# First three batches by halves of d_ff, float64 weights converted in pairs, G in float32 on quarters of the array

## The chip, the core and the metric

The kernel runs on one core of a Trainium2 chip. The core has five engines with a queue each: TensorE (PE in the profile, its weight loads PEld), VectorE (DVE), ScalarE (ACT), GpSimd (POOL) and SyncE (SP), which here issues every DMA. The metric is the device time of one execution in microseconds (us); less is better.

## The reference

Inputs are float64 weights and float32 activations. Eight batches b of 512 tokens, 8 heads of 64, and 32 state rows per head and batch:

```python
scores  = scale * x @ state.T                 # per batch and head
xread   = softmax(scores)  @ state            # 512 token rows a batch
sread   = softmax(scores.T) @ x               # 32 state rows a batch
x1 = concat([xread, sread])                   # 8 * 544 rows of 512
y  = relu(x1 @ w_in1)**2 @ w_out1             # d_ff = 2048, "MoE 1"
out = silu(y @ w_in2) @ w_out2                # "MoE 2"
```

## The kernel before, in words

**Folding.** For the token rows the kernel never forms xread. It multiplies the state by the first weight: G = state @ w_in1 per batch and head, so that x1 @ w_in1 becomes softmax(scores) @ G. The softmaxed scores, transposed, are the pages AThi/ATlo; G's are Ghi/Glo. Accurate products are made from float32r halves: hi*hi + hi*lo + lo*hi, three matmuls in place of one.

**Weights.** They come as pairs of 32-bit words (the float64's halves, int32 page `raw`). A piece is 128 rows by 512 columns, its raw page 512 KB. `c_load` fetches it, `c_abs` (ACT) and `c_bits` (five DVE instructions of 512 columns: three TENSOR_SCALAR, two SCALAR_TENSOR_TENSOR) rebuild two float32 parts a and c in the page `cv`, and `c_split` (one ACT cast, two TENSOR_TENSOR) makes hi and lo of their sum. For the second MoE's weights `c_sum` adds a and c and `c_store` keeps the float32 sum in DRAM. Each 512 x 2048 weight is 16 pieces. The first weight is converted twice, the second time (`w1s`, its rows in another order) for the state rows.

**G.** `g_unit(i)` takes piece i (column block q = i // 4, row block p = i % 4) and four block matrices `sp` of the state (128 x 128, half of it zeros, built hi and lo by `sp_build`). For each `sp`, which serves two batches, three float32r matmuls of 512 columns go to one PSUM bank; ACT or DVE copies it to the page `go`. G of batches 0 and 1 goes straight into their Glo pages by DMA, that of 2 to 7 to DRAM (`g_d`), from where `G_load` fetches it and `G_split` (ACT cast, DVE subtraction of 1024 columns) makes hi and lo.

**Stage A** has 144 slots, (batch j, block c of 128 columns of d_ff): j = 0 to 7 with 512 tokens each, and j = 8 with the 256 state rows. In a slot `gemm1` makes h in psC (6 matmuls for a token batch), `chain_a` makes relu and square and splits it (`rg`, `gact`: ACT, one DVE subtraction), and two slots later `gemm2` adds it into the four banks psA and psB (4 x 3 matmuls). So a token slot has 18 matmuls of 512 columns. After a batch's 16 slots `evac_a` copies the four banks out. Scores of a batch take two float32 matmuls a half g for batch 0 (`sblkf`), and six float32r ones (`sblk`, `x_split`) for the others; softmax work and the read of the state rows (`sread`) are spread over earlier and later slots. Batches 0 and 1 have their `sread` put off to slots 16 to 26.

**Stages after A** multiply by the second MoE's weights in a seven-product scheme (`gemm3`, `gemm4`); the change does not touch them.

**Order.** Nothing is issued as written. Each call is recorded by the class `Plan` (`record`, line 140; all instructions therefore show line L184) with an estimated cost (`cost`, line 107). `order` plays the program through with these costs, picks by urgency among the operations of the next 25 slots, respects the 50 pages of 128 x 1024 float32 in SBUF, and `emit` issues the result. Every engine then runs its own queue in that fixed order. `arith` may go to DVE or POOL and `copy` to ACT or DVE, as the plan decides. Functions that the change touches: `cost` 107, `c_load` to `sched_conv` 479 to 531, `g_unit` 571, `G_load` 596, `scores` 624, `sread_evac` 738, `gemm2` 772, `evac_a` 783, `sched_attention` 1067, `init` 1089, and the schedule in lines 1101 to 1176.

## Time and profile before

| | us |
|---|---|
| median of 3 runs | 1411.97 |
| lowest and highest run | 1406.2, 1414.91 |
| the profiled execution, its own time | 1404.88 |
| its span, first to last instruction | 1403.0 |

The profiled execution is 7.1 us (0.5%) under the median, and 1.9 us of its time lie outside the span. The profile's first part gives each engine's busy time; "windows" give it for stretches of the span, with instruction counts; groups of instructions give a mean duration; the order of time ("timeline") merges neighbours of one kind and gives in brackets what ended an idle stretch before them. The durations of instructions on one engine overlap a little, and a matmul's recorded duration runs from its start to the modelled end of its pipeline, so the distance between starts is what one costs in a stream. PEclk is the granted TensorE clock, 1.00 being 2.4 GHz.

### The profile page before, as it was taken

The page shows a single profiled execution, that of the slowest core. Times are in us where ns is not written, and L with a number is a line of the kernel's source. Part 1 is how long each engine was busy: PE and PEld are TensorE (multiplying, and loading weights), DVE is VectorE, ACT ScalarE, POOL GpSimd, SP SyncE. Part 2 cuts the span into 40 slices and gives each one's busy share as a digit, 9 for nine tenths or more (in the row PEclk, how much of TensorE's full clock was granted, in tenths as well). Part 3 has the DMA queues.
Part 4 walks back from the last instruction along what each step waited for, and adds up shares of the span by engine and source line. Part 5 has one row for each costly group of instructions (what it writes and reads, how often), then busy time and mean ns, then how long its engine had stood idle before and what let it go on. Part 6 is the DMA issues. An engine that isn't in the chain of part 4 may idle for free. (4 is left out here: it accounts for less than half of the span.)

```text
span 1403.0 us, 21067 instructions
## 1 busy us (share of the span) xinstructions
PE 1360.8 (97%) x7764; PEld 1187.9 (85%) x7764; DVE 1059.6 (76%) x1711; ACT 728.8 (52%) x1156; POOL 46.0 (3%) x41
## 2 busy tenths in 40 slices
PE   6888899999999999999999999999999999999998
PEld 3566688888888888888997888998889999999998
DVE  8999997888888888888888867777887444445443
ACT  8875674655565655566762534244555333333331
POOL 2000000000000000000021000000100000000000
PEclk9999999999999999999999999999999999999999
DMA  9981152545464636541738966677899666665563
GB/s 359 367 323 45 40 148 76 172 136 180 128 186 126 198 103 196 167 166 44 241 111 305 363 226 233 243 245 263 296 329 333 218 198 220 214 191 193 188 191 110
DMA packets 205943, 283.20 MB, mean 202 GB/s; under 512 B 12432, under 2 KB 147088, under 8 KB 205840
## 3 DMA queue, kind: packets, MB, share of 16 engines
q1 hardware_dynamic: 205840, 281.85, 60.6%
q8 instruction: 61, 1.00, 0.3%
q14 instruction: 42, 0.34, 0.1%
HBM read 165.54 MB, written 112.07 MB: 198 GB/s over the span
## 5 line engine op out<-in xcount | busy, mean ns | idle before, releaser
L184 ACT ACTIVATE rg<-psC 128x512 f32<-128x512 f32 (+1 forms) x144 | 82.4, 574 | 178.3 <-PE psC L184 177.0
L184 DVE TENSOR_TENSOR gact<-rg,gact 128x512 fp32r<-128x512 f32 (+1 forms) x142 | 93.3, 657 | 25.8 <-ACT rg L184 23.5
L184 DVE SCALAR_TENSOR_TENSOR cv<-raw,cv 128x512 int32<-128x512 int32 (+1 forms) x160 | 109.4, 688 | 0.9
L184 PE MATMUL psC<-AThi,Ghi 128*128 128x512 f32 x256 | 100.6, 398 | 2.3 <-ACT rg L184 1.7
L184 DVE TENSOR_SCALAR cv<-cv 128x512 int32<-128x512 int32 (+1 forms) x240 | 98.0, 426 | 4.4 <-ACT cv L184 3.4
L184 PE MATMUL psC<-AThi,Glo 128*128 128x512 f32 x256 | 100.0, 395 | 0.0
L184 PE MATMUL psC<-ATlo,Ghi 128*128 128x512 f32 x256 | 99.5, 393 | 0.0
L184 ACT ACTIVATE gact<-rg 128x512 fp32r<-128x512 f32 (+1 forms) x144 | 87.6, 608 | 3.4
L184 PEld LDWEIGHTS psC<-AThi,Ghi 128*128 128x128 f32 x256 | 47.9, 188 | 15.6 <-ACT rg L184 4.3
L184 ACT ACTIVATE cv<-raw 128x512 f32<-128x512 f32 x80 | 53.0, 671 | 8.4 <-DMA raw<-in_w_dram 5.5
L184 PEld LDWEIGHTS psC<-AThi,Glo 128*128 128x128 f32 x256 | 48.0, 188 | 10.8 <-DVE Glo L184 0.4
L184 PEld LDWEIGHTS psC<-ATlo,Ghi 128*128 128x128 f32 x256 | 48.1, 188 | 10.5
L184 DVE TENSOR_TENSOR rg<-rg 128x512 f32<-128x512 f32 (+1 forms) x52 | 34.3, 660 | 27.6 <-ACT rg L184 27.1
L184 ACT ACTIVATE rg<-rg 128x512 f32<-128x512 f32 (+1 forms) x92 | 54.8, 595 | 0.0
L184 ACT ACTIVATE r<-r 128x1024 f32<-128x1024 f32 (+2 forms) x20 | 18.7, 933 | 62.2 <-DVE r L184 54.9
L184 DVE TENSOR_TENSOR W<-psC,U 128x512 f32<-128x512 f32 (+2 forms) x40 | 24.1, 609 | 25.3 <-PE psC L184 25.2
L184 DVE TENSOR_TENSOR Glo<-Glo,Ghi 128x1024 fp32r<-128x1024 f32 x32 | 39.0, 1218 | 1.1 <-ACT Ghi L184 1.0
L184 ACT ACTIVATE W<-W 128x1024 f32<-128x1024 f32 (+2 forms) x20 | 18.7, 933 | 36.8 <-DVE W L184 31.6
L184 ACT ACTIVATE U<-U 128x512 f32<-128x512 f32 (+2 forms) x36 | 28.6, 796 | 14.1 <-DVE U L184 13.9
L184 ACT ACTIVATE r<-psA 128x512 f32<-128x512 f32 (+2 forms) x40 | 20.8, 533 | 28.5 <-PE psA L184 28.4
L184 DVE TENSOR_TENSOR U<-psB,U 128x512 f32<-128x512 f32 (+2 forms) x40 | 23.8, 606 | 13.9 <-PE psB L184 10.8
L184 ACT CAST Ghi<-Glo 128x1024 fp32r<-128x1024 f32 x32 | 33.4, 1045 | 0.5 <-DMA g<-go 0.5
(1422 smaller groups left out, 4575.4 us busy)
## 6 DMA issues: line engine op xcount, KB each, us to landing
raw<-in_w_dram SPq DMA_DIRECT2D x64, 512.0 KB, 6.4
t<-s SPq DMA_DIRECT2D x36, 512.0 KB, 5.2
Glo<-g SPq DMA_DIRECT2D x48, 256.0 KB, 4.4
t<-r SPq DMA_DIRECT2D x24, 512.0 KB, 4.4
xTr<-in_xT_dram SPq DMA_DIRECT2D x16, 512.0 KB, 5.7
g<-go SPq DMA_DIRECT2D x16, 512.0 KB, 6.5
xnr<-in_xN_dram SPq DMA_DIRECT2D x16, 512.0 KB, 5.1
x<-yt SPq DMA_DIRECT2D x32, 256.0 KB, 4.0
```

Source lines behind the costliest of these rows:

```text
L184: lambda engine=engine, method=method, a=a, k=k: getattr(engine, method)(*a, **k)))
```

## The change

It does the following, all in the preparation and in stage A.

1. The slots of batches 0, 1, 2 run in two parts: c 0 to 7 of batch 0, 1, 2 (slots 0 to 23), then c 8 to 15 of the same (24 to 47); from slot 48 on batches 3 to 8 as before. After a first part `evac_part` copies the four banks into two pages, after the second `y_add` adds the banks to them (4 DVE additions instead of copies).
2. Conversions work on two pieces at once: 1024-column pages a and c. Where DVE reads the raw words (SCALAR_TENSOR_TENSOR) and in `c_abs` it stays at 512 columns an instruction.
3. The first weight is not split: `c_sum` makes it one float32 page. `g_unit` multiplies it with the float32 state as loaded, in 64 x 64 quarters: per unit 8 float32 matmuls (64 rows, 64 columns of weights, 512 columns moving) at the array positions (0,0), (64,64), (0,64), (64,0). The `sp` matrices go. Column blocks q = 0, 1 (units 0 to 7) are made ahead of slot 0, blocks q = 2, 3 (units 8 to 15) at slot 17, between batch 1's and batch 2's first part, since they use the banks psA and psB.
4. The converted first weight is stored in DRAM (`w1_d`, 8 x 512 KB) and fetched and split for the state rows, in place of the second conversion.
5. Scores of batches 1 and 2 also go in float32 (two matmuls a half), without `x_split` and `sblk`.
6. `sread` of batches 0, 1, 2 is put off to slots 34 to 50; `w3`/`w4` conversions, in pairs, to slots 50 to 134. A unit's Glo pieces are sent by 4 DMAs instead of 2, `G_load` takes 4 instead of 2, `sread_evac` 8 transposes of 32 x 32 instead of 4 of 32 x 64.
7. The plan's cost takes a quarter matmul at a fourth.

```diff
-            return max(n / 2.4 + 13, 109) * (4 if args["rhs"].dtype == F32 else 1)
+            share = 4 if args.get("tile_position") else 1
+            return max(n / 2.4 + 13, 109) * (4 if args["rhs"].dtype == F32 else 1) / share
...
-    A_END = (B + 1) * NC
     N_PAGE, N_QUAD = 50, 10
+    NB, ST, PARTS = 3, 34, ((0, 8), (8, 16))
...
+    w1_d = [dram_tile([P, 1024], f"w1d{i}") for i in range(NC // 2)]
...
-    g_d = [[dram_tile([4 * P] + k + [512], f"g{i}{q}") for q in range(4)] for i, k in enumerate(([], [2]))]
+    g_d = [[dram_tile([4, P] + k + [512], f"g{i}{q}") for i, k in enumerate(([], [2]))] for q in range(4)]
...
+    def c_load(key, srcs):
+        raws[key] = [page("raw", I32) for _ in range(2)]
+        for t, src in zip(raws[key], srcs):
+            D.dma_start(t, src)
...
+        a = page("cv", F32)
+        for k in range(2):
+            A.activation(out=a[:, k * 512:(k + 1) * 512], in_=words(key, k)[1].bitcast(F32), func=AF.Abs)
...
+        a, c = cv[key], page("cc", F32)
+        ai, ci = a.bitcast(I32), c.bitcast(I32)
...
         V.tensor_scalar(out=a, in0=a, scalar1=UP_LO, scalar2=UP_HI, op0=ALU.max, op1=ALU.min)
...
+        for k in range(2):
+            h = slice(k * 512, (k + 1) * 512)
+            V.scalar_tensor_tensor(out=ci[:, h], in0=words(key, k)[1], scalar=-0x40000000, in1=ai[:, h],
+                                   op0=ALU.bitwise_and, op1=ALU.bitwise_or)
...
+        V.tensor_scalar(out=ai, in0=ci, scalar1=-0x800000, scalar2=None, op0=ALU.bitwise_and)
+        for k in range(2):
+            h = slice(k * 512, (k + 1) * 512)
+            V.scalar_tensor_tensor(out=a[:, h], in0=words(key, k)[0].bitcast(U32), scalar=2.0 ** -52, in1=a[:, h],
+                                   op0=ALU.mult, op1=ALU.mult)
...
-    def c_sum(key):
+    def c_sum(key, into=None):
         a, c = cv[key]
         arith(ALU.add, c, c, a)
         cv[key] = c
+        if into is not None:
+            into[key] = c
...
+        hi, lo = page(f"hi{key}"), page(f"lo{key}")
+        split_into(hi, c, c)
+        arith(ALU.add, lo, c, a)
+        into[key] = (hi, lo)
...
+    def sched_conv(key, srcs, s, into=None, dst=None, ahead=3, whole=False):
+        at(s - ahead, "dma", c_load, key, srcs)
         at(s - 1, "vec2", c_abs, key)
         at(s, "vec", c_bits, key)
-        if into is None:
-            at(s + 1, "vec", c_sum, key)
+        if into is None or whole:
+            at(s + 1, "vec", c_sum, key, into)
...
-    sp = [page(f"sp{i}") for i in range(4)]
-    sblkf = quad("sblkf")
+    sblkf = [quad(f"sblkf{b}") for b in range(NB)]
...
-        pg = w1p[("w1", i)]
-        rows = slice(p * P, (p + 1) * P)
-        for bp in range(4):
-            t = acc_tile(bp)
-            for k, (so, mo) in enumerate(((0, 0), (512, 0), (0, 512))):
-                T.matmul(out=t, lhsT=sp[bp][:, so + p * P:so + (p + 1) * P], rhs=pg[:, mo:mo + 512],
-                         start=k == 0, stop=k == 2)
-            if bp % 2 == 0:
-                o2 = page(f"go{i}{bp}", F32)
-            o = o2[:, bp % 2 * 512:(bp % 2 + 1) * 512]
-            copy(o, t)
+        pg = w1p[("w1", i // 2)][:, i % 2 * 512:(i % 2 + 1) * 512]
+        for bp in range(0, 4, 2):
+            ts = [acc_tile(bp), acc_tile(bp + 1)]
+            for k in range(2):
+                for r in range(2):
+                    ps, co = slice(r * 64, (r + 1) * 64), 64 * (r ^ k)
+                    T.matmul(out=ts[k][co:co + 64], lhsT=st[ps, bp + k, p].rearrange("p e n -> p (e n)"),
+                             rhs=pg[ps], start=True, stop=True, tile_position=(r * 64, co))
+            o2 = page(f"go{i}{bp}", F32).rearrange("p (k f) -> p k f", k=2)
+            for k in range(2):
+                copy(o2[:, k], ts[k])
             if bp == 0:
                 for b in range(2):
                     if (b, q) not in gp:
                         gp[(b, q)] = [None, page(f"Glo{b}{q}")]
-                    D.dma_start(gp[(b, q)][1][l * 64:(l + 1) * 64, g * 512:(g + 1) * 512].bitcast(F32),
-                                o[(b ^ l) * 64:((b ^ l) + 1) * 64])
-            elif bp == 1:
-                D.dma_start(g_d[0][q][rows], o)
-            elif bp == 3:
-                D.dma_start(g_d[1][q][rows], o2.rearrange("p (b f) -> p b f", b=2))
+                    for r in range(2):
+                        D.dma_start(f32(gp[(b, q)][1])[l * 64 + r * NS:l * 64 + (r + 1) * NS, g * 512:(g + 1) * 512],
+                                    o2[r * 64 + b * NS:r * 64 + (b + 1) * NS, 0])
+                D.dma_start(g_d[q][0][p], o2[:, 1])
+            else:
+                D.dma_start(g_d[q][1][p], o2)
+
+    def w1_store(i):
+        D.dma_start(w1_d[i], w1p.pop(("w1", i)))
+
+    def w1_load(i):
+        w1p[("s", i)] = split_page(f"w1s{i}", 1024, lambda lo: D.dma_start(lo, w1_d[i]))
     def G_load(b, q):
         lo = page(f"Glo{b}{q}")
-        src = g_d[b // 4][q]
-        src = (src[:, b // 2 % 2] if b >= 4 else src).rearrange("(g l e p) f -> l e p g f", g=2, l=2, e=2)
+        bp, e = divmod(b, 2)
+        src = g_d[q][1][:, :, bp % 2] if bp > 1 else g_d[q][0]
         for l in range(2):
-            D.dma_start(lo[l * 64:(l + 1) * 64, :].bitcast(F32).rearrange("p (g f) -> p g f", g=2),
-                              src[l, (b % 2) ^ l])
+            for r in range(2):
+                ro = (r ^ bp % 2) * 64 + e * NS
+                po = l * 64 + r * NS
+                D.dma_start(f32(lo)[po:po + NS].rearrange("p (g f) -> p g f", g=2),
+                            src.rearrange("(g l) x f -> l x g f", l=2)[l, ro:ro + NS])
         gp[(b, q)] = [None, lo]
...
-        if b == 0:
+        if b < NB:
             for l in range(2):
                 c0 = (2 * g + l) * P
-                T.matmul(out=t, lhsT=sblkf[:, c0:c0 + P], rhs=x[:, l * 512:(l + 1) * 512],
+                T.matmul(out=t, lhsT=sblkf[b][:, c0:c0 + P], rhs=x[:, l * 512:(l + 1) * 512],
...
         for h in range(4):
-            ps = slice(h * NS, (h + 1) * NS)
-            V.transpose(out=srT[ps, 2 * g:2 * g + 2, b * NS:(b + 1) * NS],
-                        in_=t[ps, h * 64:(h + 1) * 64].rearrange("p (e d) -> p e d", e=2))
-
-
-    gact, acc, yq = {}, {}, {}
+            for e in range(2):
+                ps = (h % 2) * 64 + e * NS
+                V.transpose(out=srT[ps:ps + NS, 2 * g + h // 2, b * NS:(b + 1) * NS],
+                            in_=t[h * NS:(h + 1) * NS, h * 64 + e * NS:h * 64 + (e + 1) * NS])
...
+        w = w2p[("w2", c // 2)]
...
+                T.matmul(out=acc[j][d][:, :n], lhsT=w[k][:, o:o + P], rhs=pg[:, s:s + n],
...
+    def y_copy(j, n):
+        ys = [page("y", F32)[:, :2 * n].rearrange("p (k n) -> p k n", k=2) for _ in range(2)]
+        for d in range(4):
+            copy(ys[d // 2][:, d % 2], acc[j][d][:, :n])
+        return ys
+
+    def evac_part(j):
+        if j in y_part:
+            y_add(j)
+        else:
+            y_part[j] = y_copy(j, S)
+        del acc[j]
+
+    def y_add(j):
+        for d in range(4):
+            y = y_part[j][d // 2][:, d % 2]
+            V.tensor_tensor(out=y, in0=acc[j][d], in1=y, op=ALU.add)
...
+        if j in y_part:
+            y_add(j)
+            ys = y_part.pop(j)
+        else:
+            ys = y_copy(j, n)
...
+        if b >= NB:
+            if g == 0:
+                at(s, "vec", sblk_build, b)
+            at(s, "vec", x_split, b, g)
+        elif g == 0:
+            at(s, "vec", s_put, b, sblkf[b], slice(0, 4, 3))
...
-        sched_conv(("w1", i), w_in_piece(w1, i), i - 19, w1p, ahead=3)
...
+    steps = [(b, c) for c0, c1 in PARTS for b in range(NB) for c in range(c0, c1)]
+    steps += [(b, c) for b in range(NB, B + 1) for c in range(NC)]
+    place = {x: s for s, x in enumerate(steps)}
...
+    for i in range(NC // 2):
+        q, p = divmod(i, 2)
+        if q < PARTS[0][1] // 4:
+            n = 2 * i - 4 * (PARTS[0][1] // 4) - 2
+            k = n - 3
+        else:
+            part = [u for u, (c0, c1) in enumerate(PARTS) if c0 <= 4 * q < c1][0]
+            n = slot(NB - 1, PARTS[part - 1][0]) + 1
+            k = n - 9 + 2 * p
+        sched_conv(("w1", i), w_in_pair(w1, i), k, w1p, whole=True)
+        at(max(n, k + 3) + 1, "late", w1_store, i)
         if i == 0:
-            at(-22, "dma", load_st, 0, B)
-        at(i - 16, "pe", g_unit, i)
-    for i in range(4):
-        at(-18, "vec", sp_build, i)
-    at(-14, "vec", s_put, 0, sblkf, slice(0, 4, 3))
+            at(-12, "dma", load_st)
+        at(n, "pe", g_unit, 2 * i)
+        at(n, "pe", g_unit, 2 * i + 1)
...
-        sched_conv(("w2", c), w_out_piece(w2, c), c - 1, w2p, ahead=5)
...
+    for i in range(NC // 2):
+        sched_conv(("w2", i), w_out_pair(w2, i), slot(0, 2 * i) - 1, w2p, ahead=5)
     for g in range(2):
-        sched_attention(1, g, 2 + 5 * g, True)
-        for b, s in ((0, 16), (1, 24)):
-            at(s + 2 * g - 1, "vec2", sm2_exp, b, g)
-            sched_sread(b, g, s + 2 * g)
-    for b in range(2):
+        for b in range(1, NB):
+            sched_attention(b, g, slot(b, 0) - 7 + g, True)
+        for b in range(NB):
+            at(ST + 6 * b + 2 * g - 1, "vec2", sm2_exp, b, g)
+            sched_sread(b, g, ST + 6 * b + 2 * g)
+    for b in range(NB):
         for q in range(4):
-            n = 16 * b + 4 * q
-            at(max(n - 3, 4 * q - 12), "vec", G_split, b, q)
-
-    for b in range(2, B):
+            n = slot(b, 4 * q)
+            if b >= 2:
+                at(n - 6, "dma", G_load, b, q)
+            at(n - 3, "vec", G_split, b, q)
+
...
+    for b in range(NB, B):
         for g in range(2):
-            sched_attention(b, g, 16 * (b - 1) + 8 * g - (2 if b == 2 else 0))
+            sched_attention(b, g, slot(b, 0) - 16 + 8 * g - (2 if b == NB else 0))
...
+    for i in range(NC // 2):
+        q, p = divmod(i, 2)
+        sched_conv(("w3", i), w_in_pair(w3, i), 52 + 10 * i, None,
+                   w3_d[q][2 * p * P:(2 * p + 2) * P, :].rearrange("(k r) n -> r k n", r=P))
+        sched_conv(("w4", i), w_out_pair(w4, i), 50 + 12 * i, None, w4_d[i].rearrange("k r n -> r k n"))
+
...
+    for i in range(NC // 2):
+        at(a0 - 8 + 2 * i, "dma", w1_load, i)
...
+        if s - LAG in items:
             j, c = items[s - LAG]
             n = S if j < SB else B * NS
-            gemm2(j, c, n, c == 0, c == NC - 1)
+            first, last = [c0 for c0, _ in PARTS], [c1 - 1 for _, c1 in PARTS]
+            if j >= NB:
+                first, last = [0], [NC - 1]
+            gemm2(j, c, n, c in first, c in last)
+            if c in last[:-1]:
+                evac_part(j)
```

## Rows read from the trace of the kernel before

**Rows 1.** The page's busy time of each engine: us (share of the span), instructions.
```profile
PE 1360.8 (97%) x7764; PEld 1187.9 (85%) x7764; DVE 1059.6 (76%) x1711; ACT 728.8 (52%) x1156; POOL 46.0 (3%) x41
```

**Rows 2.** Windows: stretch, its us, busy us (instructions) by engine, PEclk, DMA share, GB/s.
```profile
0.00:9.80 9.80, 0.03 (x1) 0.03 (x1) 5.12 (x10) 4.67 (x10) 5.63 (x12) 1.00 0.81 302
9.80:73.00 63.20, 55.29 (x184) 32.69 (x184) 60.85 (x128) 55.10 (x111) 6.31 (x4) 1.00 1.04 374
73.00:171.30 98.30, 85.33 (x344) 63.79 (x345) 92.99 (x177) 63.38 (x112) 2.42 (x2) 0.98 0.35 126
171.30:700.00 528.70, 528.70 (x2564) 444.39 (x2563) 451.50 (x841) 319.67 (x544) 6.33 (x9) 1.00 0.49 152
700.00:1403.00 703.00, 691.43 (x4677) 646.97 (x4675) 449.19 (x560) 286.02 (x383) 25.35 (x14) 1.00 0.70 233
```

**Rows 3.** TensorE in order of time: start, us, instruction, count, idle before.
```profile
154.24 0.73 PE L184 MATMUL psA<-gact,w('w2', 13)_434 128*128 128x512 f32 x2 [1.00 <-ACT w('w2', 13)_434 L184]
...
169.47 1.07 PE L184 MATMUL psA<-gact,w('w2', 15)_451 128*128 128x512 f32 x4
170.38 1.07 PE L184 MATMUL psB<-gact,w('w2', 15)_451 128*128 128x512 f32 x4
171.28 0.39 PE L184 MATMUL psC<-ATlo,Ghi 128*128 128x512 f32 x1
```

**Rows 4.** Groups on TensorE, 0 to 171.3 us: count, busy us, mean ns.
```profile
L184 PE MATMUL psD<-xTr,sblkf 128*128 128x512 f32 x8 | 4.2, 600 | 0.0
```

**Rows 5.** TensorE in order of time around a float32 matmul of batch 0's scores.
```profile
36.12 1.02 PE L184 MATMUL psD<-xTr,sblkf 128*128 128x512 f32 x2
36.58 1.26 PE L184 MATMUL psA<-w('w1', 6)_277,sp 128*128 128x512 f32 x3
```

**Rows 6.** Windows of the instructions that touch cv, then U: DVE, ACT (POOL) busy.
```profile
0.00:171.30 171.30, 116.92 (x224) 40.26 (x64) 0.99 0.63 227
...
0.00:171.30 171.30, 17.15 (x25) 2.52 (x4) 0.00 (x0) 0.99 0.63 227
```

**Rows 7.** Groups on VectorE by shape, 0 to 171.3 us: count, busy us, mean ns.
```profile
L184 DVE TENSOR_SCALAR cv<-cv 128x512 int32<-128x512 int32 x64 | 26.4, 422 | 0.1
L184 DVE SCALAR_TENSOR_TENSOR cv<-raw,cv 128x512 int32<-128x512 int32 x32 | 22.2, 695 | 0.0
L184 DVE SCALAR_TENSOR_TENSOR cv<-raw,cv 128x512 f32<-128x512 uint32 x32 | 22.0, 686 | 0.0
L184 DVE TENSOR_SCALAR cv<-cv 128x512 f32<-128x512 f32 x32 | 14.6, 459 | 3.2 <-ACT cv L184 3.2
L184 DVE TENSOR_TENSOR gact<-rg,gact 128x512 fp32r<-128x512 f32 x17 | 11.7, 687 | 0.4 <-ACT rg L184 0.4
L184 DVE TENSOR_TENSOR Glo<-Glo,Ghi 128x1024 fp32r<-128x1024 f32 x5 | 6.1, 1214 | 0.0
...
L184 DVE TENSOR_TENSOR ATlo<-AT,AThi 128x512 fp32r<-128x512 f32 x4 | 2.7, 686 | 0.0
...
L184 DVE RECIPROCAL sm<-sm 128x16 f32<-128x16 f32 x4 | 1.0, 248 | 0.0
...
L184 DVE TENSOR_TENSOR w('w1', 4)_264<-cv 128x512 fp32r<-128x512 f32 x1 | 0.7, 691 | 0.0
```

**Rows 8.** Start of the span on ScalarE, in order of time.
```profile
4.48 0.67 ACT L184 ACTIVATE cv<-raw 128x512 f32<-128x512 f32 x1 [2.46 <-DMA raw<-in_w_dram]
```

**Rows 9.** VectorE's transposes of the state rows, 171.3 to 700 us.
```profile
L184 DVE STREAM_TRANSPOSE srT<-psD 32x64 f32<-32x64 f32 x64 | 15.7, 245 | 6.8 <-PE psD L184 5.9
```

**Rows 10.** SyncE's queue in order of time: start, us of issuing, count.
```profile
22.57 1.11 SPq L184 DMA_DIRECT2D Glo<-go  x2
...
24.43 0.86 SPq L184 DMA_DIRECT2D g<-go  x2
```

**Rows 11.** ScalarE's copies of G out of PSUM, 0 to 171.3 us.
```profile
L184 ACT COPY go<-psB 128x512 f32<-128x512 f32 x32 | 17.5, 607 | 1.0 <-PE psB L184 1.0
```

More of the change, by code (lines that the diff above doesn't have):

```diff
@@ L445, in att_tile @@
         return BD[n_att[0] % 2]
+    f32 = lambda ap: ap.bitcast(F32)
     def arith(op, o, a, b):
@@ L462, in split, with split_page @@
         return hi
+    def split_page(key, size, load):
+        lo, hi = page(f"{key}lo"), page(f"{key}hi")
+        load(f32(lo))
+        split_into(hi[:, :size], lo[:, :size], f32(lo)[:, :size])
+        return hi, lo
     ev = defaultdict(list)
@@ L531, in sched_conv, with w_in_pair, w_out_pair, st_of @@
             at(s + 2, "late", c_store, key, dst)
-    def w_in_piece(w, i):
-        q, p = divmod(i, 4)
-        return w.bitcast(I32)[p * P:(p + 1) * P, q * 1024:(q + 1) * 1024]
-    def w_out_piece(w, c):
-        return w.bitcast(I32)[c * P:(c + 1) * P, :]
-    st = plan.tile(pages, [P, B, 4, NS], F32, "page", "st")
+    def w_in_pair(w, i):
+        q, p = divmod(i, 2)
+        return [w.bitcast(I32)[r * P:(r + 1) * P, q * 1024:(q + 1) * 1024] for r in (2 * p, 2 * p + 1)]
+    def w_out_pair(w, i):
+        return [w.bitcast(I32)[c * P:(c + 1) * P, :] for c in (2 * i, 2 * i + 1)]
+    st = plan.tile(pages, [P, 4, 4, 2, NS], F32, "page", "st")
     sblk = [page(f"sblk{i}") for i in range(2)]
-    sp = [page(f"sp{i}") for i in range(4)]
-    sblkf = quad("sblkf")
+    sblkf = [quad(f"sblkf{b}") for b in range(NB)]
     ident = plan.tile(const, [P, P], F32, "ident", "ident")
     srT = plan.tile(pages, [P, 4, B * NS], F32, "page", "srT")
+    def st_of(b, r):
+        return st[r * 64:(r + 1) * 64, b // 2, :, b % 2].rearrange("p (g l) n -> p g l n", l=2)
     def s_build(b, dst, a):
@@ L757, in gemm1 @@
             o = (c % 4) * P
-            ops = [(w1p[("s", c // 4 * 4 + k)][:, wo + o:wo + o + P], a[:, k * 256:(k + 1) * 256])
-                   for k in range(4) for wo, a in ((0, ahi), (512, ahi), (0, alo))]
+            ops = [(w1p[("s", c // 4 * 2 + k // 2)][w][:, k % 2 * 512 + o:k % 2 * 512 + o + P], a[:, k * 256:(k + 1) * 256])
+                   for k in range(4) for w, a in ((0, ahi), (1, ahi), (0, alo))]
         for i, (w, a) in enumerate(ops):
@@ L901, in w4_split @@
         split_into(hi, lo, f32(lo))
-    def split_page(key, size, load):
-        lo, hi = page(f"{key}lo"), page(f"{key}hi")
-        load(f32(lo))
-        split_into(hi[:, :size], lo[:, :size], f32(lo)[:, :size])
-        return hi, lo
     def x_op(u, i):
@@ L1143, in attn_moe_moe_kernel @@
+    a0 = slot(SB, 0)
     at(a0 - 2, "vec", s_tokens_split)
-    for i in range(NC):
-        sched_conv(("s", i), w_in_piece(w1s, i), a0 - 12 + i, w1p)
+    for i in range(NC // 2):
+        at(a0 - 8 + 2 * i, "dma", w1_load, i)
     at(a0 + 6, "vec", w3_build, 0)
@@ L1151, in attn_moe_moe_kernel @@
     LAG = 2
-    items = [(j, c) for j in range(B + 1) for c in range(NC)]
+    items = dict(enumerate(steps))
+    A_END = max(items) + LAG + 1
     first_slot = min(s for s, _ in ev)
-    for s in range(first_slot, A_END + LAG + 2):
+    for s in range(first_slot, A_END):
         plan.slot = s
         fire(s, "dma")
-        if 0 <= s < A_END:
+        if s in items:
             j, c = items[s]
@@ L1174, in attn_moe_moe_kernel @@
         fire(s, "late")
+    for s in range(A_END, A_END + 2):
+        fire(s, "dma")
     assert not ev, sorted(ev)
-    base = A_END + LAG + 2
+    base = A_END + 2
     for u in range(NU):
```

100 lines of the change are left out of this document (29 added, 71 removed).

## The prediction

> **What bounds the kernel now.** I read the page's busy times first: TensorE 97%, VectorE 76%, nothing else near [rows 1]. An average says little here, so I cut the span into windows next. From 171.3 to 700 us TensorE is busy for 528.7 of 528.7 us, and it is nearly so to the end; before that it is not [rows 2]. The reader is to see two regimes: a start in which something else limits, and 1230 us in which only fewer or cheaper matmuls would help.
>
> Then I counted what the start should have cost. In a stream the starts of four matmuls of 512 columns lie 0.91 us apart, so one costs 0.226 us [rows 3]. At 171.3 us the last gemm2 group of batch 0 has been issued [rows 3]. Until then the windows hold 1 + 184 + 344 = 529 TensorE records [rows 2]; 8 of them are passes of float32 matmuls [rows 4], 521 are the 512-column kind: 521 x 0.226 = 117.7 us. A float32 matmul is two passes: two take 1.02 us and one alone 0.60, so their distance is about 0.43 us [rows 4, 5], and 8 cost 3.4 us. Work 121.2, so **50.1 us of the first 171.3 are lost**. This is all that a better start could win.
>
> Who holds TensorE up? VectorE is busy for 60.85 of 63.2 us and 92.99 of 98.3 us there, 96% and 95% [rows 2], and TensorE's gaps end with a converted weight [rows 3]. Of VectorE's work the conversions are 116.9 us [rows 6]. So both weights' conversions must pass through VectorE before batch 0 is through, while TensorE has one batch to work on.
>
> **The change part by part.** The sum is made against the profiled execution (1404.9 us, 7.1 under the median of 1412.0) and the difference is then taken off the median.
>
> *Conversions in pairs.* A piece costs VectorE three TENSOR_SCALAR (0.42, 0.46, 0.42), two SCALAR_TENSOR_TENSOR (0.69) and two TENSOR_TENSOR (0.69) [rows 7], together 4.06 us; 32 pieces make 130 us against 116.9 of busy time, since neighbours overlap: factor 0.90 [rows 6]. No row has a TENSOR_SCALAR of 1024 columns: it lies between the 0.42 of 512 columns and twice that. TENSOR_TENSOR goes from 0.69 to 1.21 with the doubling [rows 7], so 0.17 of it does not grow; with that 0.17, 0.42 becomes 0.68, which I take. A pair of the first weight: 3 x 0.68 + 4 x 0.69 + one sum 1.21 = 6.0, times 0.90 = 5.5 us (before 7.3). A pair of the second, with two TENSOR_TENSOR: 6.6 us. The bounds shift a pair by 0.7 us down and 0.4 up.
>
> *Halves of d_ff.* Before slot 8 VectorE now needs 4 pairs of the first weight (22.0), batch 0's softmax, two G splits (2 x 1.1), 4 pairs of the second weight (26.4) and 8 chain subtractions (8 x 0.62): a softmax half is six instructions on U at 0.69 (17.15 us for 25 [rows 6]), one subtraction 0.62 and two small ones at most 0.22 each [rows 7], so 10.4 a batch. Sum 66.0; at 96% busy 68.6. ScalarE begins at 4.48 us and needs 0.67 for each of a pair's two pieces [rows 8], so VectorE starts at 5.9: batch 0's first part ends at **74.5 us** or later. From there through the second G stretch VectorE needs 22.0 + two softmaxes 20.8 + four splits 4.4 + 5.0 = 52.2, at 96% 54.4: 128.9 us.
>
> *G in float32 quarters.* It removes 192 matmuls x 0.226 = 43.4 us and adds 128 quarter matmuls, each two passes. No row shows a quarter. From below: four run side by side, 0.86 / 4 = 0.215 us each. From above: they run one after the other, 0.86. I take **0.43**, by the float32 rows, the nearest: the queue is in order, the second pass starts when the first has streamed, and the instruction queued behind it starts no earlier than the second pass [rows 5]. So the next quarter's first pass can join the current one's second, and never more than two passes are in flight. 128 x 0.43 = 55.0: +11.6 us. Half of it (27.5) lies in VectorE's shadow ahead of slot 8; the other half, at slot 17, is bare, as psA and psB are taken for it and all gemm2 of batch 2 is queued behind. The 32 bank copies of that stretch (0.6 each [rows 11]) take 19 us of ScalarE, beside it.
>
> The Trainium skill, "TensorE: Matmul & The Clock Gate", Part 3, says that matmuls start and end in program order and that weight loads alone are pulled ahead; by it the price is the 0.43 taken. No row here has two tiles in the array, so the trace can't confirm it for quarters.
>
> *Changing between whole array and quarters.* No row shows its price. From below nothing; from above the part of a pass that the next one normally hides, 0.60 - 0.43 = 0.17 [rows 4, 5], at both ends of 16 groups: 5.4 us. I take 2, as few other matmuls are ready at slot 17. The Trainium skill, "TensorEngine Tiling (Array Packing)", Key Properties, says that switching the mode drains the engine, which speaks for a price above zero; no row shows it.
>
> *Sum for TensorE.* To slot 8: 27.5 + 3.4 + 8 slots x 18 x 0.226 (32.5) = 63.4 us of work against 74.5: 11.1 idle. Then 32.5 + two batches' scores 6.9 + 27.5 = 66.9 against VectorE's 54.4: TensorE bounds, nothing is lost. Hand-offs will cost something beside the floor; I take 15 idle (11 to 25). *Scores* of batches 1 and 2: 16 passes x 0.43 against 24 x 0.226: +1.5. Difference: idle 15 - 50.1, G +11.6, scores +1.5, changes +2 = **-20.0 us**.
>
> *At nothing, with their cover.* The second conversion of the first weight goes (16 x 3.7 us of VectorE) and 8 splits of 1.1 come: it lies where TensorE is busy throughout [rows 2], so nothing is won. The same cover hides 64 transposes more (at most 64 x 0.245 us [rows 9]), 12 additions and copies at part ends, and the later w3/w4 conversions: VectorE is at 85% there [rows 2]; without that cover, part ends would cost some 2 us each, three times. The 4 MB written and read for `w1_d` replace 8 MB of raw words.
>
> *SyncE.* A unit has 4 Glo DMAs and 2 to `g_d`. At 1.11 / 2 and 0.86 / 2 us each [rows 10] that is 3.1 us, for 8 units 24.6 us, within the 27.5 us of the stretch at slot 17. Queued behind them, and behind their waits for the copies, are the raw words of the second weight's last four pairs, first needed at slot 24, when gemm2 of batch 2's part (8 x 12 x 0.226 = 21.7 us) is over. `G_load`'s 48 DMAs more are spread over 500 us.
>
> **The rivals.** *Four abreast.* If quarters share the array fully, G costs 27.5 in all, -15.9. VectorE then bounds to 128.9 plus the last pair's two units 3.4, against work of 102.9: 29.4 idle, say 30. -50.1 + 30 - 15.9 + 1.5 + 2 = -32.5: **1379.5**. For it: the four positions never share rows and a bank's partitions at once. Against: the in-order pairs of passes. It gives less than G saves because VectorE stays the floor. The Trainium skill, "TensorEngine Tiling (Array Packing)", Key Properties, says that tiles operate independently and load and multiply in parallel; by that this rival would be the outcome.
>
> *Slower: quarters one at a time.* At 0.86 G costs 110, +66.6. It is TensorE that then bounds the start (first unit at 5.9 + 5.5 = 11.4 us, then 55 + 3.4 + 32.5), with 12 idle: 12 - 50.1 + 66.6 + 1.5 + 2 = +32: **1444**. It decides from 0.61 us a quarter matmul on, where the sum is nil (128 p = 43.4 + 50.1 - 12 - 1.5 - 2 = 78). For it: no row has any overlap of streaming passes. Against: quarters use different rows and columns.
>
> *The pool of pages.* At slot 17 some 44 of the 50 pages are held: second weight 8, scores 6, halves of y 4, G 8, copies 4, first weight 4, chain 7, three fixed. A pair's conversion in flight takes 6. If pages keep the first weight's second half from being converted under batch 1, the stretch starts one pair late: 4.5 to load, 1.3 and 5.7 to convert, 11.5 us, of which gemm1 of batch 2 (10.8) may cover none. At 10 of it: -10, **1402**, no change that can be told. For it: the count. Against: the plan knows the pool and can order around it.
>
> **How the numbers follow.** Two abreast 0.42, four abreast 0.28, pages 0.18, one at a time 0.12. The likeliest: 1412.0 - 20 = **1392 us** (1385 by the profiled execution); its own range with 11 to 25 idle and 0 to 5.4 for changes is 1386 to 1405. The range reaches down to four abreast with cheaper TENSOR_SCALAR (16 pairs, half of the 0.7 us on the path: 1372) and up past the page case to 1414; left out are most of the slow rival and the tails. About 1% (14 us) is what can be told from no change. Faster by more: three quarters of the first (0.32), all of the second, a little of the third: 0.61. Slower by more: 0.12 and a tail, 0.14. Between: 0.25.
>
> **What would show it.** Right: float32 quarter passes with starts about 0.215 us apart on average (two abreast); batch 0's first part ending at 75 to 80 us and the stretch at slot 17 lasting 27 us; TensorE idle of some 15 us ahead of it; 1024-column TENSOR_SCALAR at 0.68. Passes 0.11 apart mean four abreast, 0.43 one at a time. TensorE gaps ended by a w2 page after slot 24 would show the pages. The sum is wrong if full-rate work after 171 us has gained gaps, which I cost at nothing.

## The result and the profile after

After: **1394.49 us** (median of 4 runs, 1393.57 to 1396.56); before, with one run more than the three of its table (1406.77): 1409.37 us. Ratio 0.9892, 95% interval 0.9855 to 0.993: about 15 us faster, where 20 were forecast (1392, range 1372 to 1414; the forecast starts from the table's 1412.0). The time was met, but of the way to it half was wrong, and two large errors cancelled: that is luck.

The profiled execution took 1396.56 us, the longest of its runs, while that of before lies under its median; so the spans differ by 8.2 us only (1403.0 and 1394.8), and stages are compared below by marks in them.

The page's busy times and the windows, as in [rows 1] and [rows 2]:

```profile
PE 1350.0 (97%) x7820; PEld 1169.2 (84%) x7820; DVE 1006.7 (72%) x1524; ACT 693.0 (50%) x1070; POOL 44.8 (3%) x42
```

```profile
0.00:9.80 9.80, 0.00 (x0) 0.00 (x0) 2.74 (x5) 3.93 (x5) 3.88 (x11) 1.00 0.80 291
9.80:73.00 63.20, 52.73 (x244) 27.22 (x245) 53.26 (x82) 46.15 (x84) 0.00 (x0) 0.97 0.90 319
73.00:171.30 98.30, 90.07 (x414) 60.62 (x413) 77.52 (x130) 58.99 (x106) 0.92 (x2) 0.95 0.48 167
171.30:700.00 528.70, 528.70 (x2626) 447.12 (x2625) 440.54 (x776) 311.26 (x524) 19.18 (x16) 1.00 0.48 153
700.00:1394.00 694.00, 678.51 (x4540) 634.20 (x4538) 432.66 (x535) 272.64 (x353) 20.84 (x13) 0.99 0.70 235
```

VectorE went from 96% and 95% busy to 84% and 79% in the two windows of the start. TensorE is hardly less idle: its first instruction comes at 14.6 us instead of 9.8.

**Where the time came from.** Slot 24 is a mark that both kernels share: 24 equal slots are behind it, 120 ahead. Its first RELU, before and then after, in ScalarE's order of time:

```profile
203.22 0.60 ACT L184 ACTIVATE rg<-psC 128x512 f32<-128x512 f32 x1
```

```profile
180.83 0.60 ACT L185 ACTIVATE rg<-psC 128x512 f32<-128x512 f32 x1 [1.68 <-PE psC L185]
```

The windows up to there, before and then after:

```profile
0.00:203.20 203.20, 172.55 (x690) 123.33 (x691) 187.45 (x370) 147.34 (x273) 16.64 (x20) 0.99 0.62 219
```

```profile
0.00:180.80 180.80, 152.29 (x699) 95.70 (x700) 141.74 (x226) 116.74 (x207) 4.80 (x13) 0.96 0.67 236
```

The groups on TensorE in that window of after give the float32 passes (the third row are the scores):

```profile
L185 PE MATMUL psB<-cc,st 64*64 64x512 f32 x128 | 27.5, 643 | 0.0
L185 PE MATMUL psA<-cc,st 64*64 64x512 f32 x128 | 26.1, 687 | 14.6 <-DVE cc L185 14.6
...
L185 PE MATMUL psD<-xTr,sblkf 128*128 128x512 f32 x24 | 13.2, 639 | 3.7 <-issue 2.4 <-ACT Sc L185 1.3
```

And the order of time shows what a quarter costs:

```profile
23.17 0.59 PE L185 MATMUL psD<-xTr,sblkf 128*128 128x512 f32 x1
23.70 1.09 PE L185 MATMUL psA<-cc,st 64*64 64x512 f32 x8
24.61 1.04 PE L185 MATMUL psB<-cc,st 64*64 64x512 f32 x8
25.57 0.70 PE L185 MATMUL psD<-xTr,sblkf 128*128 128x512 f32 x1
```

The same group, with the view ended at 23.90, so that only its first starts are in it:

```profile
23.70 0.66 PE L185 MATMUL psA<-cc,st 64*64 64x512 f32 x4
```

Eight passes, so four quarter matmuls, take 0.91 us (23.70 to 24.61): four passes start together, and the four second ones behind them. **Four run abreast.** Two rounds of 0.43, four at once, make 0.86, or 0.107 us a pass and 0.215 a quarter matmul. The 0.05 left over belongs to the change from the whole array (in the doubled run below, where group follows group, it is gone). TensorE's work up to slot 24 is then, after, 256 x 0.107 + 24 x 0.43 + 419 x 0.226 = 132.4 us of 180.8: **48.4 lost**. Before: 8 x 0.43, 48 smaller instructions of the state reads (some 5 us, estimated by their columns) and 634 x 0.226, together 151.7 of 203.2: **51.5 lost**. So the lost time hardly fell (-3.1); TensorE has less to do (G -16.0, scores +1.5). Lost is not all idle: by the busy column TensorE stands still for 28.5 us of these 180.8 (before 30.7 of 203.2), and some 6 us are lost to the slower clock (estimated below, with the doubled run). The reads, some 5 us, only moved behind slot 24, where they cost their time again.

ScalarE's first copy in `gemm3`, before and then after, lies 16.3 us earlier, which is -3.1 - 16.0 + 1.5 and about 1 us more lost in between:

```profile
720.97 0.59 ACT L184 COPY U<-psA 128x512 f32<-128x512 f32 x1 [0.78 <-PE psA L184]
```

```profile
704.69 1.07 ACT L185 COPY U<-psA 128x512 f32<-128x512 f32 x2 [1.00 <-PE psA L185]
```

**Given back later.** From that copy to the end it is 682.0 us before and 690.1 after. TensorE's waits from 690 us on, before and then after (what it waited for: us in total, times, longest):

```profile
PE psA L184 <- ACT u L184: 4.3, 5, 2.0
PE psA L184 <- ACT U L184: 1.3, 1, 1.3
```

```profile
PE psA L185 <- ACT u L185: 4.7, 5, 2.0
PE psD L185 <- DVE g070lo L185: 3.5, 1, 3.5
PE psC L185 <- ACT g050hi L185: 1.7, 1, 1.7
```

The two `g0..` waits stand where `gemm3` gives way to `gemm4`; they are new. The window there has the clock at 0.77, where it was 1.00 before ([rows 2], 700 to 1403 us):

```profile
1046.00:1061.00 15.00, 12.11 (x82) 12.11 (x83) 9.77 (x9) 4.76 (x6) 0.00 (x0) 0.77 0.86 307
```

The 8.1 us are a difference of two single executions, and that of before lies 4.5 us under its median. Set against the 14.9 us between the medians, only some 1.4 of the 16.3 are lost again; how many they are is open, the waits are not.

### The profile page after: what moved, and what is told of

It is laid out like the page before. It is cut to its first block, busy times and chain, and to the rows that moved or that the text cites. A ratio compares the mean times of both kernels' runs of the same rounds, so it can differ in the third digit from the quotient of the medians.

```text
span 1394.8 us, 21037 instructions
## 1 busy us (share of the span) xinstructions
PE 1350.0 (97%) x7820; PEld 1169.2 (84%) x7820; DVE 1006.7 (72%) x1524; ACT 693.0 (50%) x1070; POOL 44.8 (3%) x42
## 5 line engine op out<-in xcount | busy, mean ns | idle before, releaser
L185 DVE TENSOR_TENSOR gact<-rg,gact 128x512 fp32r<-128x512 f32 (+1 forms) x139 | 90.8, 655 | 20.4 <-ACT rg L185 14.6
L185 DVE TENSOR_TENSOR rg<-rg 128x512 f32<-128x512 f32 (+1 forms) x66 | 43.7, 662 | 50.5 <-ACT rg L185 50.3
L185 PEld LDWEIGHTS psC<-AThi,Glo 128*128 128x128 f32 x256 | 48.2, 188 | 14.6 <-issue 2.1
L185 DVE TENSOR_SCALAR cv<-cv 128x1024 f32<-128x1024 f32 (+1 forms) x64 | 43.3, 685 | 8.0 <-ACT cv L185 7.7
L185 ACT ACTIVATE rg<-rg 128x512 f32<-128x512 f32 (+1 forms) x78 | 46.3, 594 | 0.0
L185 ACT ACTIVATE cv<-raw 128x512 f32<-128x512 f32 x64 | 40.6, 667 | 7.3 <-DMA raw<-in_w_dram 6.3
L185 DVE SCALAR_TENSOR_TENSOR cc<-raw,cv 128x512 int32<-128x512 int32 x64 | 41.8, 683 | 3.3 <-DMA g<-go 3.1
L185 DVE SCALAR_TENSOR_TENSOR cv<-raw,cv 128x512 f32<-128x512 uint32 x64 | 41.6, 683 | 0.2
L185 PE MATMUL psA<-cc,st 64*64 64x512 f32 x128 | 26.1, 687 | 14.6 <-DVE cc L185 14.6
```

The lines of the kernel that those rows point to most:

```text
L185: lambda engine=engine, method=method, a=a, k=k: getattr(engine, method)(*a, **k)))
```

## The experiments

Each is the changed kernel with one edit. The marks below come from the profiled executions: first RELU of slot 16 and of slot 24, first copy of `gemm3`, and from there to the end of the span (us). Ratios are to the kernel before on the same chip; its median differs between the four chips used by up to 3 us (1406.57 to 1409.55), so times of different chips compare to that accuracy only. Every edit makes the plan order everything anew: a run measures the edit together with its new order.

| kernel | slot 16 | slot 24 | gemm3 | to the end | median | ratio, 95% interval |
|---|---|---|---|---|---|---|
| before | | 203.2 | 721.0 | 682.0 | 1409.37 | |
| after | 132.0 | 180.8 | 704.7 | 690.1 | 1394.49 | 0.9892, 0.9855 to 0.993 |
| e1_no_halves | | 187.3 | 710.9 | 686.2 | 1400.04 | 0.9935, 0.9912 to 0.9957 |
| e2_double_rounds | 127.0 | 185.8 | 709.6 | 689.0 | 1399.55 | 0.9934, 0.9911 to 0.9957 |
| e3_double_same_quarter | 128.7 | 187.8 | 711.4 | 687.7 | 1401.74 | 0.9959, 0.994 to 0.9977 |
| e4_g_on_pool_queue | 132.6 | 181.4 | 705.3 | 689.1 | 1396.15 | 0.991, 0.9886 to 0.9935 |
| e5_light_conversion | 118.3 | 166.4 | 690.3 | 682.0 | 1376.86 | 0.978, 0.9753 to 0.9806 |
| e6_single_width | 135.1 | 184.7 | 708.4 | 690.4 | 1399.64 | 0.9943, 0.9925 to 0.9961 |
| e7_split_scores | 140.4 | 184.8 | 708.6 | 681.7 | 1393.39 | 0.9901, 0.9862 to 0.994 |
| e8_convert_twice | 132.6 | 181.5 | 705.7 | 688.4 | 1394.75 | 0.9911, 0.9884 to 0.9938 |
| e9_sum_on_pool | 135.8 | 184.7 | 708.6 | 691.0 | 1400.33 | 0.9936, 0.9916 to 0.9955 |
| e10_sums_on_pool | 138.8 | 187.7 | 711.6 | 686.4 | 1400.62 | 0.9947, 0.992 to 0.9974 |
| e11_after_again | 132.3 | 181.2 | 706.2 | 686.4 | 1394.54 | 0.9899, 0.9873 to 0.9925 |
| e12_sum_in_psum | 124.7 | 183.2 | 707.4 | 690.6 | 1399.65 | 0.9929, 0.9906 to 0.9952 |

**The halves undone.**

```diff
-    NB, ST, PARTS = 3, 34, ((0, 8), (8, 16))
+    NB, ST, PARTS = 3, 34, ((0, 16),)
-    at(-14, "vec", init)
+    at(-24, "vec", init)
-            at(-12, "dma", load_st)
+            at(-22, "dma", load_st)
```

> The changed kernel, but batches 0 to 2 run their 16 slots whole: all 16 G units stand ahead of slot 0. Theory (the halves give VectorE time): before slot 16 VectorE then needs 8 pairs of the first weight, one softmax, four splits, 8 pairs of the second and 16 subtractions, 44 + 10.4 + 4.4 + 52.8 + 9.9 = 121.5 us, at 96% busy and with the start 132, against 96 us of matmuls to that point at four quarters abreast; so 36 us idle by that floor where the halves have 30, and some 10 us later than the changed kernel in all: about 1404. Rival (the matmuls saved by quarters are the whole gain, the halves give nothing): 1394, within 3 us of the changed kernel.

Measured 1400.04: the halves are worth about 5.5 us, neither nothing nor the whole change. Slot 24 comes 6.5 us later. (With the halves goes the place of G's second part: all 16 units stand ahead of slot 0.)

**G's quarter matmuls doubled**, each group of four issued a second time (A B C D A B C D, the letters standing for the positions (0,0), (64,64), (0,64), (64,0)).

```diff
-            for k in range(2):
+            for k in (0, 1, 0, 1):
```

> Each group of four quarter matmuls is issued twice (A B C D A B C D, same result): G's time in the array doubles from 27.5 to 55 us, which is what two abreast would have cost. Theory (the G units ahead of slot 0 lie in VectorE's shadow, the 8 units at slot 17 are bare, but there the copies out of PSUM already take 19 us against 13.7): plus 8 to 14 us, 1403 to 1409. Rival (all of G is on the path): plus 27, 1422.

TensorE's order of time: a doubled group takes 1.71 us, 0.215 a quarter matmul. So G costs 55 us here, just the price that the prediction had taken.

```profile
20.27 1.89 PE L185 MATMUL psA<-cc,st 64*64 64x512 f32 x16
21.98 1.89 PE L185 MATMUL psB<-cc,st 64*64 64x512 f32 x16
```

27 us more of matmuls made the kernel 5 us slower. The marks say where: slot 16 comes 5.0 us *earlier*, and from slot 16 to 24, where G's second half lies, it takes 58.8 us instead of 48.8. The first half costs nothing in VectorE's shadow, the second is bare. The windows to slot 16, of this kernel and then of after, and three short ones of after:

```profile
0.00:127.00 127.00, 107.33 (x564) 67.39 (x565) 114.13 (x180) 80.00 (x140) 5.25 (x13) 1.00 0.67 236
```

```profile
36.85:40.27 3.42, 3.42 (x18) 0.83 (x18) 3.42 (x10) 1.45 (x4) 0.00 (x0) 0.50 0.75 222
88.05:94.88 6.83, 4.95 (x12) 3.35 (x12) 6.83 (x11) 0.67 (x2) 0.00 (x0) 0.50 0.00 0
125.60:129.01 3.41, 3.41 (x9) 2.64 (x8) 3.41 (x7) 1.21 (x2) 0.00 (x0) 0.50 0.00 0
0.00:132.00 132.00, 103.49 (x436) 65.32 (x437) 113.51 (x178) 80.79 (x143) 4.80 (x13) 0.95 0.63 227
```

In after, TensorE is granted 1.2 GHz for 13.7 us in three stretches of the start, which it does not fill (103.49 of 132.0 us busy); with the doubled matmuls it keeps 2.4 GHz. It is busy for 11.8 of them (3.42 + 4.95 + 3.41), so by estimate half of that, 5.9 us, is the price, enough to pay for the 5.0. That it does was not tried by itself; the plan's new order is a rival. Up to slot 24 the doubled kernel has 132.4 + 27.4 = 159.8 us of work in 185.8: 26 lost instead of 48.4. **The idle time is what the start leaves TensorE, not a sum of hand-offs**: with more work it shrinks.

**The same doubling, each quarter matmul written twice in a row.**

```diff
+                    for _ in range(2):
                         T.matmul(out=ts[k][co:co + 64], ...
```

> The same doubled work as in the kernel with each group issued twice, but each quarter matmul is repeated at once (A A B B C C D D). Theory (TensorE keeps strict order: a matmul waits for its quarter, and everything behind it waits too): only two matmuls overlap, a doubled group takes 4 x 0.86 = 3.4 us instead of 1.7, G 110 us, and the stretch at slot 17 alone grows by 27 us or more: 1430 or later. Rival (quarters have queues of their own, a waiting quarter does not hold up the others): the same time as with rounds A B C D, within 3 us.

```profile
21.95 1.95 PE L185 MATMUL psB<-cc,st 64*64 64x512 f32 x16
23.66 2.14 PE L185 MATMUL psA<-cc,st 64*64 64x512 f32 x16
```

Again 1.71 us a doubled group, but this does not decide, for A A B B C C D D was not what ran. The plan counts 3 ns from a matmul to the next on the same output (`LATENCY`, pe to pe) and issues what is ready first, so all 32 groups went out as A B A B C D C D. In a long row of these, strict order would give 1.71 us as well: the second A B beside C D, the second C D beside the next A B. What decides is a group that follows a whole-array matmul. By strict order only A and B start there, and C and D 0.86 us later, behind the second A and B. The view ended at 42.62:

```profile
42.03 0.59 PE L185 MATMUL psD<-xTr,sblkf 128*128 128x512 f32 x1
42.55 0.67 PE L185 MATMUL psA<-cc,st 64*64 64x512 f32 x4
```

Four first passes start within 0.04 us, so C and D went ahead of the second A and B: while a quarter is busy with its first matmul, the one waiting behind it does not hold up the other quarters.

**G's DMAs on GpSimd's queue.**

```diff
-                D.dma_start(g_d[q][1][p], o2)
+                DG.dma_start(g_d[q][1][p], o2)        (and the five other issues of a unit)
```

> The DMAs that send G from its copies (Glo pieces and the two stores) are issued by GpSimd instead of SyncE, in the same planned order. Theory (in SyncE's one queue the raw words of the next pairs stand behind G's DMAs, which wait for their copies; VectorE is only 84% busy from 9.8 to 73 us for that): raw words land earlier, minus 3 to 8 us, 1386 to 1391. Rival (VectorE's own order and its waits for ScalarE and TensorE set the start): no change, 1394 within 3.

No change beyond the intervals (0.991 and 0.9892): SyncE's queue does not set the start.

**VectorE relieved.**

```diff
+            if key[0] in ("w3", "w4"):
                 V.scalar_tensor_tensor(out=a[:, h], in0=words(key, k)[0]..., scalar=2.0 ** -52, ...)
```

> Left out: for the first MoE's weights (and so in the output) the low words' SCALAR_TENSOR_TENSOR, two a pair. VectorE then has 16 x 1.2 = 19 us less to do in the first 180 us, 10 of them ahead of the end of batch 0's first part. Theory (VectorE's queue sets the start; the doubled G cost only 5 us of 27, so TensorE has slack there): minus 8 to 12 us, 1383 to 1387. Rival (latencies of the hand-offs between DMA, ScalarE, VectorE and TensorE set it, VectorE being 84% busy): within 3 us of 1394.5.

17.6 us faster (15.8 by the ratios), 14.4 of them at slot 24 and kept to `gemm3`, and the rest behind it. This is the strongest sign that VectorE sets the start. The clock stays at 1.00 here too, so the 14.4 may hold some of its price (5.9 by the estimate above). And the two instructions left out also lie on the way of each pair to TensorE: the run doesn't tell VectorE's load from the length of that way.

**Conversions 512 columns wide** (every 1024-column conversion instruction written as two).

```diff
-        V.tensor_scalar(out=a, in0=a, scalar1=UP_LO, ...)
+        for h in hs:
+            V.tensor_scalar(out=a[:, h], in0=a[:, h], scalar1=UP_LO, ...)
```

> Conversions still handle a pair, but every VectorE and ScalarE instruction on it has 512 columns: per pair three TENSOR_SCALAR more (2 x 0.42 for 0.68) and one or two TENSOR_TENSOR more. That is 0.5 + 0.17 us a pair of the first weight and 0.5 + 0.34 of the second before overlap, some 8 us over the 12 pairs needed by slot 17. Theory (VectorE sets the start): plus 4 to 8 us, 1398 to 1402. Rival (it does not): within 3 us of 1394.5.

1399.64, 5.1 slower (7.2 by the ratios), at slot 24 3.9: the wider instructions give some 4 to 7 us.

**Scores of batches 1 and 2 in float32r halves again.**

```diff
-        if b < NB:
+        if b < 1:
```

> Scores of batches 1 and 2 again from float32r halves: 24 matmuls of 0.226 us for 16 passes of 0.43, and four x_split (1.2 us of VectorE, 1.0 of ScalarE each) and two sblk builds come back. Theory (VectorE sets the start): 1.5 us less for TensorE, 5 to 6 more for VectorE, so plus 2 to 5 us, 1396 to 1400. Rival (float32 scores cost TensorE more than they save): minus 1 to 2 us.

1393.39, no difference that the intervals allow; 3.9 us later at `gemm3`, and that won back behind it. Float32 scores neither give nor cost anything in the whole.

**The first weight converted twice**, nothing kept in DRAM.

```diff
-        at(max(n, k + 3) + 1, "late", w1_store, i)
-        at(a0 - 8 + 2 * i, "dma", w1_load, i)
+        sched_conv(("s", i), w_in_pair(w1, i), a0 - 12 + 2 * i, w1p)
```

> The first weight is not kept in DRAM but converted and split a second time for the state rows (8 pairs, 6.6 us of VectorE each, where TensorE is busy throughout). Theory (hidden, as predicted at nothing): within 3 us of 1394.5. Rival (VectorE's relief there is part of the gain, for instance by letting the next stage's weights be built earlier): plus 4 us or more.

1394.75: the second conversion is hidden, and keeping the weight is worth nothing.

**The first weight's sums on GpSimd, then the second's last sums as well.**

```diff
-        arith(ALU.add, c, c, a)
+        G.tensor_tensor(out=c, in0=c, in1=a, op=ALU.add)
...
-        arith(ALU.add, lo, c, a)
+        G.tensor_tensor(out=lo, in0=c, in1=a, op=ALU.add)      (second run only)
```

> The changed kernel, but the sum of the first weight's low parts (one TENSOR_TENSOR of 1024 columns a pair) always goes to GpSimd instead of to the engine the plan picks (VectorE in the start). Theory (VectorE's work sets the start, about one to one): the light conversion took 19 us of VectorE's work away and won 17.6; here up to 8 x 1.21 = 9.7 us leave VectorE, but GpSimd needs about 1.3 us for 512 columns, so some 2.6 us a sum, and the pair is later by that. I take 5 to 9 us gained: 1386 to 1390, first copy of gemm3 at 696 to 700 us of the profiled run. Rival (the hand-over on GpSimd is itself on the path, or GpSimd slows VectorE's accesses): 1394 to 1400, with VectorE idle behind GpSimd's sums in the first 100 us.

> As the run before, and the second weight's last sum goes to GpSimd as well: up to 16 x 1.21 = 19.4 us off VectorE, as much as the light conversion left out (19 us, -17.6), but without leaving out any result. Theory (VectorE alone sets the start): 1378 to 1386. Rival (GpSimd's 2.6 us a sum come into the path of each pair, since the plan keeps only few pairs in flight): no better than the run with the first weight's sums alone.

Both theories of a gain fell: 1400.33 and 1400.62, 6 us slower. Groups up to 100 us (count, busy us, mean ns): GpSimd's sums in the first of the two runs, VectorE's rows in the same run, VectorE's in the second run, and last VectorE's in after:

```profile
L185 POOL TENSOR_TENSOR cc<-cc,cv 128x1024 f32<-128x1024 f32 x4 | 11.0, 2739 | 24.1 <-DVE cv L185 24.1
```

```profile
L185 DVE SCALAR_TENSOR_TENSOR cc<-raw,cv 128x512 int32<-128x512 int32 x19 | 14.5, 794 | 2.3 <-DMA g<-go 2.3
```

```profile
L185 DVE SCALAR_TENSOR_TENSOR cc<-raw,cv 128x512 int32<-128x512 int32 x16 | 12.6, 816 | 0.5 <-DMA g<-go 0.4
...
L185 DVE TENSOR_SCALAR cv<-cv 128x1024 int32<-128x1024 int32 x10 | 8.7, 882 | 0.1
...
L185 DVE TENSOR_TENSOR Glo<-Glo,Ghi 128x1024 fp32r<-128x1024 f32 x3 | 5.4, 1786 | 0.0
```

```profile
L185 DVE SCALAR_TENSOR_TENSOR cc<-raw,cv 128x512 int32<-128x512 int32 x20 | 12.9, 684 | 3.1 <-DMA g<-go 3.1
...
L185 DVE TENSOR_SCALAR cv<-cv 128x1024 f32<-128x1024 f32 x10 | 6.8, 685 | 7.0 <-ACT cv L185 7.0
L185 DVE TENSOR_SCALAR cv<-cv 128x1024 int32<-128x1024 int32 x10 | 6.7, 680 | 0.0
...
L185 DVE TENSOR_TENSOR cc<-cc,cv 128x1024 f32<-128x1024 f32 x4 | 4.9, 1215 | 0.0
L185 DVE TENSOR_TENSOR Glo<-Glo,Ghi 128x1024 fp32r<-128x1024 f32 x3 | 3.6, 1202 | 0.0
...
L185 DVE TENSOR_TENSOR U<-U,sm 128x512 f32<-128x512 f32 x4 | 2.7, 698 | 0.0
```

A sum takes 2.74 us on GpSimd against 1.22 on VectorE, and a pair is late by the difference. Beside it VectorE's instructions stretch: the mean goes from 684 to 816 ns, from 680 to 882, from 1202 to 1786. The stretch is not even. In the first of the two runs, GpSimd's first sum and VectorE's two instructions beside it:

```profile
13.29 2.72 POOL L185 TENSOR_TENSOR cc<-cc,cv 128x1024 f32<-128x1024 f32 x1 [8.79 <-DVE cv L185]
```

```profile
13.12 3.44 DVE L185 SCALAR_TENSOR_TENSOR cc<-raw,cv 128x512 int32<-128x512 int32 x2
```

One of the two takes 0.68 us, the other, which begins under the sum, 2.84. The Trainium skill, "SBUF — State Buffer", section "SBUF: two separate sides", says that a VectorE instruction with two inputs in SBUF and a GpSimd instruction that reads SBUF hold a shared pair of ports in turn, each for a whole instruction; an instruction that grows by about the length of a sum agrees with it.

**The changed kernel once more.**

> The changed kernel unchanged, for a second profiled execution: 1394.5 within 2 us. If the loss at the entry to gemm4 comes from the planned order, first copy of gemm3 to first z lies 370 +- 2 us apart again and TensorE waits for VectorE's g070lo conversion again. If it came with that one execution, the distance is 364 to 367 us and the wait is gone.

1394.54, with slot 24 at 181.2 and 369.6 us from the first copy of `gemm3` to VectorE's first z out of psD, as after (370.7; before, in its one execution, 364.4). TensorE waits 3.4 us for `g070lo` again, and the clock is at 0.77 again from 1046 to 1061 us. So the loss at `gemm4`'s entry belongs to the planned order. The light conversion and the split scores, planned otherwise, wait only 1.0 and 1.4 us for `g070lo`, keep the clock at 1.00 there and take 682.0 and 681.7 to the end. Why the plan puts the `g0..` conversions late is open.

**The sum left to TensorE**, from the kernel that converts twice.

```diff
-        pg = w1p[("w1", i // 2)][:, i % 2 * 512:(i % 2 + 1) * 512]
+        a, c = (t[:, i % 2 * 512:(i % 2 + 1) * 512] for t in w1p[("w1", i // 2)])
...
-            for k in range(2):
+            for k, pg in ((0, c), (1, c), (0, a), (1, a)):
...
-                             rhs=pg[ps], start=True, stop=True, ...
+                             rhs=pg[ps], start=pg is c, stop=pg is a, ...
```

> From the kernel that converts the first weight twice (1394.75): in the first pass the two parts of a converted pair are not added on VectorE (8 TENSOR_TENSOR of 1024 columns, 1.216 us each, 9.7 us); G is computed from each part and TensorE adds them in the banks, so every quarter matmul is issued twice, on c and on a. Theory (VectorE's work sets the start about one to one, TensorE's G price at 0.18 per us): -9.7 x 0.93 + 5 = -4: 1389 to 1393, first copy of gemm3 about 4 us earlier than with the sum on VectorE. Rival 1 (the page that holds the second part longer, or the added passes, set the start): 1396 to 1402. Rival 2 (the sum's latency and hand-over were on the path of each pair too, 8 times some 1.5 us): 1380 to 1386.

1399.65, in rival 1's range; the gain did not come. By the ratios it is only 2.5 us behind the kernel that it came from, and the intervals overlap. The marks show how the two effects stand to each other: slot 16 comes 7.9 us earlier than in the kernel that it came from (124.7 and 132.6), with VectorE spared 9.7 us and more work that keeps up the clock, and from 16 to 24 it takes 58.5 us against 48.9, which is G's doubled second half in the open. Doing this for the first eight units only was not tried.

No run that leaves nothing out was faster than after by more than the intervals.

## Why the prediction was right, and where it was wrong

**VectorE bounds the start: right.** With VectorE relieved of 19 us of work, slot 24 came 14.4 us earlier, part of which may be the clock's; with 27 us more work for TensorE it came 5.0 later. Whether it is VectorE's load alone, or also the hand-offs of each pair between DMA, ScalarE, VectorE and TensorE, the runs do not separate.

**The price of the quarters: wrong.** The step "I take 0.43 ... So the next quarter's first pass can join the current one's second, and never more than two passes are in flight" failed: the first passes of four quarters start together, and a quarter costs 0.215 us, the lower bound. G changed TensorE's work by -16.0, not +11.6: 27.6 us too dear. The float32 row of the whole array was the nearest row but the wrong likeness; the order in one array says nothing of the order among quarters. The Trainium skill's rule on program order ("TensorE: Matmul & The Clock Gate", Part 3) did not give that price: taken for whole matmuls, it lets A B C D start together. I had applied it to the single passes. It does not hold here either: in the run with the matmuls written twice in a row, C and D started ahead of the second A and B (four starts within 0.04 us). The Trainium skill's rule that tiles operate independently ("TensorEngine Tiling (Array Packing)", Key Properties) fits: 0.91 us for four.

**"I take 15 idle (11 to 25)": wrong**, 48.4 lost in the same sense, 33 too little. Two things failed in it. First, idle time is no term of its own: it is VectorE's pace less TensorE's work, and when G came out 27 us cheaper the idle time rose with it; at the price that I had taken for G, which the doubled run has, 26 are lost. *Four abreast* had this mechanism and the quarters right, but with 30 idle its 1379.5 is 15 too low. Second, the pace. The amount of VectorE's work was right: 66.0 + 52.2 = 118 us were counted, and 113.5 are done at slot 16. But it is 86% busy there, not 96% (some 6 us pass before the first words are there, and it waits for a DMA, 3.1 us in the groups of after above, and for banks and casts). And behind it come 19 us that I had laid beside VectorE's work, the second stretch of G. After, the copies in the window 135 to 155 us ([rows 11] answer to them):

```profile
L185 ACT COPY go<-psA 128x512 f32<-128x512 f32 x13 | 7.2, 590 | 1.5 <-PE psB L185 0.9 <-PE psA L185 0.6
L185 ACT COPY go<-psB 128x512 f32<-128x512 f32 x12 | 6.9, 592 | 3.1 <-PE psA L185 1.7 <-PE psB L185 1.4
```

The stretch lasts 19 us (forecast 27), with 13.7 of quarter passes, and VectorE is busy for 4.93 of 19.5 us in it:

```profile
135.50:155.00 19.50, 19.50 (x136) 6.20 (x135) 4.93 (x8) 14.78 (x29) 0.00 (x0) 1.00 0.63 207
```

So the two errors, -27.6 for G and +32 for the lost time (it fell by 3.1, not by 35.1), cancelled to within 5 us, and -17.6 took the place of -20. That the sum came out is luck.

**Batch 0's first part at 74.5 us or later: it ended at 99.** The floor holds, but the plan had VectorE do ten pairs and two batches' softmax by then (the rows x10 and `U` x4, two halves a batch, among the groups of after above), where I counted eight and one. No time hangs on it, since the 24 slots are what counts.

**TENSOR_SCALAR of 1024 columns at 0.68, the sum at 1.21: right** (0.68 and 1.22 in the rows above). **Changes of mode at 2: right in size.** In the order of time above, a change to quarters and back costs 0.10 on entering (23.17 to 23.70 is 0.53 against 0.43), 0.05 in the first group (0.91 against 0.86) and 0.10 on leaving (24.61 to 25.57 is 0.96 against 0.86). G lies in twelve stretches between whole-array matmuls, so some 3 us by estimate. Between groups of quarters in a row nothing is lost (two in 1.71 us). **Scores +1.5: right, and without effect. The second conversion at nothing: right. SyncE's queue: right. The pool of pages: no sign of it**; no wait of TensorE in the start names a second-weight page after slot 24.

**"The sum is wrong if full-rate work has gained gaps, which I cost at nothing"**: it has, 5 to 6 us up to VectorE's first z out of psD in the two profiled executions (370.7 and 369.6 against 364.4 in the one of before). I had no step for it, as the change does not touch that stage; the plan that orders all stages together does.
